# The end of a whole block of an expert, moved from ahead of the branch into both of its arms

## The chip, the cores and the metric

One core of a Trainium2 chip runs the whole program: TensorE (PE, with its weight loads as PEld), VectorE (DVE), ScalarE (ACT), GpSimd (POOL) and the queue of transfers of SyncE (SP). The metric is the device time of one launch in microseconds, the median of several launches.

## The reference

Attention with keys and values that are averaged over 8 rows, then two layers of experts (mixture of experts) over 4608 rows of 512 numbers. The first layer sends each row to its two best of 8 experts, the second to its best one. An expert is two matrix products with a ReLU between them.

```python
def _moe_ref(x, w_gate, w_noise, noise, w1, w2) -> np.ndarray:
    ...
    top2 = np.argpartition(-noisy_logits, 2, axis=1)[:, :2]
    ...
    for e in range(E):
        for k in range(2):
            mask = top2[:, k] == e
            if not mask.any():
                continue
            h = np.maximum(x[mask] @ w1[e], 0.0)
            out[mask] += top2_w[mask, k, None] * (h @ w2[e])

def _moe2_ref(x, w_gate, w_output_gate, w1, w2) -> np.ndarray:
    ...
    e_idx = np.argmax(logits, axis=1)
    ...
        h = np.maximum(x[mask] @ w1[e], 0.0)
        ye = h @ w2[e]
        out[mask] = gate_w[mask, None] * eom[mask, e, None] * ye
```

## The kernel before

The first 250 us are the attention and the routing of the first layer; they are not touched. Then 16 experts run one after the other (k = 0 to 7 in the first layer, 8 to 15 in the second), each through `region(k)`. How many rows an expert has is known only on the chip, so its rows run in **whole blocks** of 256 rows, as nested branches: `level(j)` is the j-th whole block, and `deeper(j)` asks with `tc.If(reg["m"] > more_than(j + 1))` (L1445) whether one more follows. If so, the if-arm holds `level(j + 1)`; if not, the else-arm holds only weight work that is left over (`rest`), or is empty. A remainder of over 192 rows counts as a whole block. Behind all levels three more branches (L1454, L1457, L1460) choose the **part block**: none, or one of up to 64, 128 or 192 rows. The branch at L1445 is announced to PE, ACT, DVE and SP at the start of each whole block by `hint(j)` (L1410); the three of the part block are not announced, and no branch is announced to POOL.

A whole block (`block` with rows == PAIR) stands in this order. `head` copies the rows' places and issues the load and the gather of the next block's rows (`nxt`: SP loads `metaN`, L760, then POOL gathers `xg`, L766). The first layer's product runs in four groups (`m1_pair`, L936), each ended by ACT and DVE (L944, L945). Then come the second product of rows 0 to 127 (`m2(k, 0)`, L998, 24 matmuls), the transposes of the next block's rows (`t_pe`, L868, ended by `t_ev`: L874 on ACT, L875 on DVE), the eviction of the first half (`y_ev`, with a write by POOL, L1027), and then the part that this change is about: the second product of rows 128 to 255 (`m2(k, 1)`, 24 matmuls), beside it on DVE some products with the gate of the second layer (`dot`, L1062, the list `own`), in the second whole block of an expert also the ranks (`rank2`), the row numbers for the write of the second half (`didx`, L1272) and `leave` (ACT L1056, L1057, DVE L1059). The second half itself is evicted at the start of the next block (`y_last`).

The gate products of a block's first half that its own `own` does not reach are done by the next block: `own` holds `OWN[min(j, 2)]` of 8 (3, 4, 6 by level), a whole block starts at `done = OWN[min(j, 3) - 1]`, and a part block at `min(OWN)` = 3, whatever the block ahead did. They are done in the experts 1 to 7 alone.

PE, ACT, DVE and SP run in the order in which the code issues; POOL's order is the scheduler's. Engines wait for each other by counters, one for each engine, that each instruction raises when it is done. The number of raises must be the same on every path through a branch, so that an arm that leaves instructions out raises the counter by what is missing, behind a wait that all earlier work of its own engine is done.

Of the kernel before, what the change touches and what calls it, by code (L numbers as in the profile page):

```python
# [25 lines left out]
E = 8  # L26
# [10 lines left out]
NT = 5  # L37
# [656 lines left out]
PAIR = 256  # L694
# [14 lines left out]
OWN = (3, 4, 6)  # L709


class Weights:
# [64 lines left out]
class Moe(Weights):  # L777
# [353 lines left out]

    def block(self, k, rows, j, nxt, last, extra, places, mid=None, z=True, turned=False):

# [4 lines left out]
        first, calm = j == 0, j > 1  # L1138
        done = OWN[min(j, 3) - 1] if rows == PAIR else min(OWN)
        col = 5 if moe == 0 else 1  # L1140
# [107 lines left out]
        if rows == PAIR:  # L1248
            if nxt is not None:
                if not gate:  # L1250
                    self.t_ev()
                if moe == 1:
                    self.z_dots(e)
            more(places[5])
            if calm:
                more(99, own)
            else:
                more(BEFORE, own)
            self.m2(k, 1, self.t_pe if turned else self.rank2_pe if pend and not calm else None, 7 if turned else 5)
            if turned:  # L1260
                self.t_ev()
                self.z_dots(e)
            if pend and not calm:
                self.rank2(own)
            more(99, own)
        elif rows == PAIR - QUART:
            more(places[5])
            self.m2_rest(w2, 1, self.rank2_pe if pend else None)
            if pend:
                self.rank2(between)  # L1270
            more(99, between)
# [111 lines left out]
    def region(self, k):  # L1383
# [28 lines left out]
        def level(j):  # L1412
# [22 lines left out]
            else:  # L1435
                def some(rows):
                    self.block(k, rows, j, lambda: self.fetch(moe, self.next_row(moe, e, j), self.c.scat[-4 * NT:] if k == 0 and j == 1 else ()), last,
                               plan[j] if j < 2 else [], places.get(j, [0] * 6), mid if first else None)
                if not first:
                    hint(j)  # L1440
                some(PAIR)
            deeper(j)

        def deeper(j):
            with tc.If(reg["m"] > more_than(j + 1), label=f"whole{k}_{j + 1}") as cmp:  # L1445
                level(j + 1)
            rest = sum(plan[j + 1:], [])
            if rest:
                with cmp.Else():
                    for f in rest:  # L1450
                        f()
# [133 lines left out]
```

## Time and profile before

| | |
|---|---|
| runs | 1708.25, 1708.44, 1714.56 us (median 1708.44) |
| profiled execution | 1712.64 us, its span 1710.9 us |
| granted TensorE clock, mean over the span | 0.968 of full speed |
| busy share of the span | PE 94%, PEld 84%, DVE 66%, ACT 41%, POOL 38% |

The page lists for each group of instructions how long its engine was idle just before it and what ended the idle time. "Issue" means that the engine waited for nothing that the profile shows. A q behind an engine's name is its sequencer, which runs ahead of the engine and takes the branches and the waits. A matmul's line has its start, then its duration.

### The profile page before, as it was taken

Reading aid. Unit: us, or ns where it says so; the run is one execution under the profiler, and the core shown is the slowest. Engines: PE = TensorE matmul, PEld = TensorE weight load, DVE = VectorE, ACT = ScalarE, POOL = GpSimd, SP = SyncE. Lnnn points to the kernel's source line nnn. Section 1 sums busy time; section 2 is a strip of 40 time slices with the busy share of each in tenths; the row PEclk is TensorE's granted clock in tenths of the full one; section 3 lists DMA queues with packets and bytes.
Section 4 is the critical chain, followed back from the end, with each engine's and each line's share of the span. In section 5 each row is a group of like instructions: output and inputs, shape, how many; then the busy total and the mean of one; then the engine's idle time right before and its main releaser. Section 6 shows DMA issues by size and latency. Waiting matters only on the chain. (4 is left out here: it accounts for less than half of the span.)

```text
span 1710.9 us, 31718 instructions
## 1 busy us (share of the span) xinstructions
PE 1600.5 (94%) x10551; PEld 1439.3 (84%) x10551; DVE 1121.5 (66%) x3941; ACT 693.4 (41%) x1388; POOL 651.9 (38%) x613
## 2 busy tenths in 40 slices
PE   7988889999999998998998999999999999899997
PEld 6878778899888898888887898888888998798886
DVE  6889874248787886886886887875444534535452
ACT  5766743252442532442532623422343423424242
POOL 4566673144354454353452553542221211112121
PEclk8988999999999999999999999999999999899998
DMA  9977865164281471562551752922423411623231
GB/s 233 266 199 216 229 204 187 58 184 114 66 215 59 120 186 57 135 159 64 154 155 54 191 143 53 248 79 71 137 86 114 147 50 61 192 74 107 91 106 32
DMA packets 148564, 226.48 MB, mean 132 GB/s; under 512 B 45090, under 2 KB 83490, under 8 KB 148128
## 3 DMA queue, kind: packets, MB, share of 16 engines
q1 hardware_dynamic: 104832, 121.67, 24.3%
q0 software_dynamic: 42368, 101.18, 22.2%
q8 instruction: 130, 2.13, 0.5%
q14 instruction: 178, 1.46, 0.3%
q10 hardware_dynamic: 1056, 0.03, 0.0%
HBM read 181.67 MB, written 54.89 MB: 138 GB/s over the span
## 5 line engine op out<-in xcount | busy, mean ns | idle before, releaser
L998 PE MATMUL yps<-w,hT 128*128 128x512 f32 x2616 | 630.7, 393 | 0.0
L936 PE MATMUL hps<-xT,w 128*128 128x256 f32 x4704 | 585.6, 286 | 22.1 <-DVEq L1454 6.8
L936 PEld LDWEIGHTS hps<-xT,w 128*128 128x128 f32 x4704 | 578.9, 194 | 32.1 <-issue 9.6
L998 PEld LDWEIGHTS yps<-w,hT 128*128 128x128 f32 x2616 | 481.5, 188 | 94.0
L1062 DVE SCALAR_TENSOR_TENSOR scr<-yb,gb 128x512 f32<-128x512 f32 x532 | 342.0, 687 | 2.7 <-DVE hT L945 1.8
L945 DVE SCALAR_TENSOR_TENSOR hT<-hps,hT 128x512 fp32r<-128x512 f32 x196 | 135.5, 691 | 229.4 <-ACT hT L944 229.3
L944 ACT ACTIVATE hT<-hps 128x512 fp32r<-128x512 f32 x196 | 117.1, 597 | 413.7 <-PE hps L936 397.5
L1027 POOL DMA_INDIRECT out_dram<-yb,didx x46 | 48.0, 1044 | 367.4 <-ACT yb L1035 306.5
L1027 POOL DMA_INDIRECT X<-yb,didx x80 | 89.4, 1118 | 239.8 <-DVE rk L1122 50.5
L766 POOL DMA_INDIRECT xg<-X,metaN x128 | 143.9, 1124 | 90.2 <-DMA metaN<-meta 36.0
L1128 POOL DMA_INDIRECT meta<-pay,sli x70 | 76.0, 1086 | 228.4 <-DMA meta<-pay,sli 111.4
L875 DVE TENSOR_TENSOR xT<-tps,xT 128x512 fp32r<-128x512 f32 x128 | 83.0, 685 | 118.5 <-ACT xT L874 118.3
L745 ACT ACTIVATE w<-stg 128x1024 fp32r<-128x1024 f32 x128 | 134.3, 1055 | 25.3 <-DMA stg<-in_moe_w_dram 25.1
L956 PE MATMUL hps<-xT,w 128*128 128x256 f32 (+1 forms) x408 | 114.1, 366 | 27.7 <-DVEq L1445 12.1
L956 PEld LDWEIGHTS hps<-xT,w 128*128 128x128 f32 x408 | 82.9, 203 | 33.2 <-issue 33.2
L874 ACT ACTIVATE xT<-tps 128x512 fp32r<-128x512 f32 x128 | 69.8, 595 | 90.3 <-PE tps L868 90.2
L751 DVE TENSOR_TENSOR w<-stg,w 128x1024 fp32r<-128x1024 f32 x68 | 82.6, 1225 | 30.5 <-ACT w L745 30.0
L958 PE MATMUL hps<-xT,w 128*128 128x128 f32 (+1 forms) x408 | 98.8, 242 | 2.2 <-issue 2.2
L529 PE MATMUL po<-Vb,AT 96*128 96x162 f32 (+1 forms) x480 | 81.6, 327 | 17.5 <-DVE Ur L554 13.3
L529 PEld LDWEIGHTS po<-Vb,AT 96*128 96x128 f32 (+1 forms) x480 | 68.5, 193 | 22.6 <-issue 15.7
L958 PEld LDWEIGHTS hps<-xT,w 128*128 128x128 f32 x408 | 84.3, 207 | 2.7 <-issue 2.7
L920 POOL DMA_INDIRECT prow<-X,pidx x70 | 76.8, 1097 | 24.4 <-issue 13.4
(279 smaller groups left out, 1846.5 us busy)
## 6 DMA issues: line engine op xcount, KB each, us to landing
stg<-in_moe_w_dram SPq DMA_DIRECT2D x128, 512.0 KB
w<-in_moe_w_dram POOLq DMA_DIRECT2D x56, 512.0 KB
vst<-in_v_dram SPq DMA_DIRECT2D x16, 576.0 KB
X<-zw SPq DMA_DIRECT2D x36, 256.0 KB
X<-xr SPq DMA_DIRECT2D x32, 256.0 KB
kst<-in_k_dram SPq DMA_DIRECT2D x14, 576.0 KB
qt<-in_q_dram SPq DMA_DIRECT2D x15, 512.0 KB
meta<-zm SPq DMA_DIRECT2D x20, 116.0 KB
```

What stands on the lines that cost most here:

```text
L529: nc.tensor.matmul(po[r, j:j + 2, :], lhsT=at[:, j, r], rhs=Vb[b % 2][:, 3 * hh + j], start=(j == 0), stop=(j == 2), skip_group_check=True)
L745: self.nc.scalar.activation(hi, self.stg[s % n], AF.Copy)
L766: return [nc.gpsimd.indirect_dma_start(out=c.xg[:, i, :], out_offset=None, in_=src, in_offset=bass.IndirectOffsetOnAxis(ap=c.metaN[:, i, 0 ...
L875: f = lambda i=i, hi=hi, lo=lo: self.nc.vector.tensor_sub(lo, self.tps[i], hi.bitcast(F32))
L936: nc.tensor.matmul(ps[:, a, :], lhsT=w[:, wi, kc, f * P:(f + 1) * P], rhs=x, start=(n == 0), stop=(n == 11))
L944: nc.scalar.activation(hi, ps, AF.Relu)
L945: nc.vector.scalar_tensor_tensor(lo, ps, 0.0, hi.bitcast(F32), op0=OP.max, op1=OP.subtract)
L956: nc.tensor.matmul(ps[a], lhsT=w[:, 0, kc, f * P:(f + 1) * P], rhs=x, start=(kc == 0), stop=False, skip_group_check=True)
L958: nc.tensor.matmul(ps[a][:, 0, :], lhsT=w[:, 1, kc, f * P:(f + 1) * P], rhs=x[:, 0, :], start=False, stop=(kc == 3), skip_group_check=True)
L998: self.nc.tensor.matmul(self.yps[i], lhsT=h, rhs=w2[:, wi, f, :], start=(f == n == 0), stop=(f == 7 and n == 2))
L1027: ins = nc.gpsimd.indirect_dma_start(out=c.out if moe else c.X, out_offset=bass.IndirectOffsetOnAxis(ap=self.didx[:, i:i + 1], axis=0), in ...
L1062: self.nc.vector.scalar_tensor_tensor((self.scr[0], self.ya if narrow else self.scr[1])[ex % 2], self.yb[:, i, :], 1.0, self.c.wgb[:, ex, ...
```

## The change

`block` gets an argument `split`. Its part from `more(99 if calm else BEFORE, ...)` to `leave` becomes a function `finish`; with `split` it is not run but returned. Levels with an ordinary whole block (all but the first whole blocks of k = 0 and k = 8, and the loop for levels from 6 on) pass it to `deeper`, which runs it first thing in the if-arm, ahead of the next level, and first thing in the else-arm. In the else-arm `finish(LEFT)` does at most 4 of the `own` products, and a part block now starts at 4 in place of 3.

```diff
+LEFT = 4
...
-    def block(self, k, rows, j, nxt, last, extra, places, mid=None, z=True, turned=False):
+    def block(self, k, rows, j, nxt, last, extra, places, mid=None, z=True, turned=False, split=False):
...
-        done = OWN[min(j, 3) - 1] if rows == PAIR else min(OWN)
+        done = OWN[min(j, 3) - 1] if rows == PAIR else LEFT
...
             more(places[5])
-            if calm:
-                more(99, own)
-            else:
-                more(BEFORE, own)
-            self.m2(k, 1, self.t_pe if turned else self.rank2_pe if pend and not calm else None, 7 if turned else 5)
-            if turned:
-                self.t_ev()
-                self.z_dots(e)
-            if pend and not calm:
-                self.rank2(own)
-            more(99, own)
+            def finish(n=E):
+                mine = own[:n]
+                more(99 if calm else BEFORE, mine)
+                self.m2(k, 1, self.t_pe if turned else self.rank2_pe if pend and not calm else None, 7 if turned else 5)
+                if turned:
+                    self.t_ev()
+                    self.z_dots(e)
+                if pend and not calm:
+                    self.rank2(mine)
+                more(99, mine)
+                nc.vector.tensor_copy(self.didx[:, 1:2], self.metaC[:, 1, col:col + 1])
+                self.leave(moe, e, halves)
+                for f in extra:
+                    f()
+            if split:
+                return finish
+            finish()
+            return
...
-                some(PAIR)
+                return deeper(j, some(PAIR))
             deeper(j)
 
-        def deeper(j):
+        def deeper(j, finish=None):
+
+            rest = sum(plan[j + 1:], [])
             with tc.If(reg["m"] > more_than(j + 1), label=f"whole{k}_{j + 1}") as cmp:
+                if finish:
+                    finish()
                 level(j + 1)
-            rest = sum(plan[j + 1:], [])
-            if rest:
+            if rest or finish:
                 with cmp.Else():
+                    if finish:
+                        finish(LEFT)
                     for f in rest:
                         f()
```

The order of instructions on two engines, for expert 1. In brackets stand the counters that an instruction waits for; `yps_3729` is the accumulator of a block's second half, `tps` and `xg` belong to the next block's rows.

**PE, from the else-arms to the part block, before.** The row with x6 is the six else-arms of the six levels, one branch each to the place behind them; no other shown instruction stands in an arm.

```order
L1445 UNCONDITIONAL_BRANCH [waits PE_49,PE_sequencer_49] x6
L1454 COMPARE_AND_BRANCH
L1457 COMPARE_AND_BRANCH
L956 MATMUL hps_3725<-xT,w_1_3682 128x256 [waits DVE_49,Activation_49]
L958 MATMUL hps_3725<-xT,w_1_3682 128x128
```

**PE, the same place, now.** The last rows of the sixth else-arm (that of the first whole block) and what follows.

```order
L1000 MATMUL yps_3729<-w_1_3683,hT_3686 128x512 x2
L1000 MATMUL yps_3729<-w_1_3683,hT_3687 128x512
L1000 MATMUL yps_3729<-w_1_3683,hT_3686 128x512
L1457 UNCONDITIONAL_BRANCH [waits PE_sequencer_49]
L1469 COMPARE_AND_BRANCH
L1472 COMPARE_AND_BRANCH
L958 MATMUL hps_3725<-xT,w_1_3682 128x256 [waits DVE_49,Activation_49]
L960 MATMUL hps_3725<-xT,w_1_3682 128x128
```

Each else-arm now holds the 24 matmuls of the second half, and its branch no longer waits for PE's own counter: the first matmul of the arm raises it by what is missing.

**PE, at the end of a level, now.** Transposes of the next block's rows, then the branch.

```order
L870 MATMUL tps_3724<-identf,xg 128x128 [waits DMASW6_49]
L870 MATMUL tps_3724<-identf,xg 128x128 x3
L1457 COMPARE_AND_BRANCH
L1000 MATMUL yps_3729<-w_1_3683,hT_3686 128x512
L1000 MATMUL yps_3729<-w_1_3683,hT_3687 128x512
```

The branch stands ahead of the second half's matmuls, where it stood behind them.

**DVE, at the end of a level, before.** L1023 is the eviction of the first half, L1062 a gate product.

```order
L1023 SCALAR_TENSOR_TENSOR yb<-prow,metaC,ya 128x512 [waits DMASW0_49,Activation_49]
L1062 SCALAR_TENSOR_TENSOR scr_3696,lg_3702<-yb,gb 128x512 [waits DVE_49]
L1062 SCALAR_TENSOR_TENSOR scr_3697,lg_3702<-yb,gb 128x512
L1062 SCALAR_TENSOR_TENSOR scr_3696,lg_3702<-yb,gb 128x512 [waits DVE_49]
L1062 SCALAR_TENSOR_TENSOR scr_3697,lg_3702<-yb,gb 128x512 [waits DVE_49]
L1062 SCALAR_TENSOR_TENSOR scr_3696,lg_3702<-yb,gb 128x512 [waits DVE_49]
L1062 SCALAR_TENSOR_TENSOR scr_3697,lg_3702<-yb,gb 128x512 [waits DVE_49]
L1272 COPY didx<-metaC 128x1 [waits DMASW5_49]
L1059 MEMSET pidx 128x2 [waits DMASW1_49]
L1445 COMPARE_AND_BRANCH
```

**DVE, an else-arm of a third or later whole block, now.** The branch L1457 of the level stands right behind the eviction of the first half (L1025).

```order
L1064 SCALAR_TENSOR_TENSOR scr_3696,lg_3702<-yb,gb 128x512 [waits DVE_49]
L1064 SCALAR_TENSOR_TENSOR scr_3697,lg_3702<-yb,gb 128x512
L1064 SCALAR_TENSOR_TENSOR scr_3696,lg_3702<-yb,gb 128x512 [waits DVE_49]
L1064 SCALAR_TENSOR_TENSOR scr_3697,lg_3702<-yb,gb 128x512 [waits DVE_49]
L1268 COPY didx<-metaC 128x1 [waits DMASW4_49]
L1061 MEMSET pidx 128x2 [waits DMASW1_49]
L1457 UNCONDITIONAL_BRANCH [waits DVE_sequencer_49]
```

Six products ahead of the branch have become four in the arm behind it (six in the if-arm). The branch at the arm's end, which waited for DVE's own counter before, waits for it no longer, and the arm's first product raises the counter by what is missing.

## Rows read from the trace of the kernel before

**Rows 1.** The page: busy us of the engines, share of the span, instructions.

```profile
PE 1600.5 (94%) x10551; PEld 1439.3 (84%) x10551; DVE 1121.5 (66%) x3941; ACT 693.4 (41%) x1388; POOL 651.9 (38%) x613
```

**Rows 2.** The page's costliest groups: busy us, mean ns | idle before, releaser.

```profile
L1062 DVE SCALAR_TENSOR_TENSOR scr<-yb,gb 128x512 f32<-128x512 f32 x532 | 342.0, 687 | 2.7 <-DVE hT L945 1.8
...
L956 PE MATMUL hps<-xT,w 128*128 128x256 f32 (+1 forms) x408 | 114.1, 366 | 27.7 <-DVEq L1445 12.1
```

**Rows 3.** Instructions of L956, the sequencer's wait ahead of a part block's first matmul.

```profile
L956 PEldq EVENT_SEMAPHORE  x14: 51/51/51, 331.9 to 1653.6; - x14
```

**Rows 4.** Timeline of PE, part block of expert 3: start, us, ..., [idle before].

```profile
675.53 0.66 PE L956 MATMUL hps<-xT,w 128*128 128x384 f32 x1 [4.33 <-issue]
...
676.15 0.58 PE L956 MATMUL hps<-xT,w 128*128 128x384 f32 x1
...
676.68 0.57 PE L956 MATMUL hps<-xT,w 128*128 128x384 f32 x1
...
680.86 0.36 PE L956 MATMUL hps<-xT,w 128*128 128x384 f32 x1
...
681.15 0.36 PE L956 MATMUL hps<-xT,w 128*128 128x384 f32 x1
...
696.66 0.17 PE L1113 MATMUL rps<-ohb,tri 128*128 128x16 bf16 x1 [0.72 <-DVE ohb L1095]
```

**Rows 5.** Instructions of L1445, 665.5 to 677 us: ns min/median/max, first and last start.

```profile
L1445 PEldq COMPARE_BRANCH  x2: 184/270/355, 667.0 to 671.5; - x2
...
L1445 DVEq COMPARE_BRANCH  x2: 47/64/80, 670.6 to 673.6; - x2
L1445 PEldq EVENT_SEMAPHORE  x2: 51/51/51, 671.2 to 671.4; - x2
L1445 DVEq EVENT_SEMAPHORE  x2: 21/21/21, 673.4 to 673.5; - x2
```

**Rows 6.** Instructions of L1460 in the same stretch.

```profile
L1460 PEldq COMPARE_BRANCH  x1: 2976/2976/2976, 672.4 to 672.4; - x1
```

**Rows 7.** Windows: us, busy PE, PEld, DVE, ACT, POOL, granted clock, DMA, GB/s.

```profile
673.91:680.74 6.83, 5.21 (x19) 5.24 (x20) 2.26 (x7) 0.66 (x2) 2.39 (x3) 0.50 0.14 46
...
919.67:926.50 6.83, 4.99 (x19) 4.99 (x20) 2.33 (x7) 0.66 (x2) 2.23 (x2) 0.50 0.14 46
```

**Rows 8.** Timeline of PE at the exits of experts 1, 5 and 12.

```profile
443.21 0.36 PE L956 MATMUL hps<-xT,w 128*128 128x256 f32 x1 [2.39 <-DVEq L1445]
...
918.86 0.41 PE L956 MATMUL hps<-xT,w 128*128 128x384 f32 x1 [2.41 <-DVEq L1445]
921.51 0.53 PE L958 MATMUL hps<-xT,w 128*128 128x192 f32 x1 [2.24 <-issue]
...
1547.56 0.36 PE L956 MATMUL hps<-xT,w 128*128 128x256 f32 x1 [1.06 <-ACT zc L907]
```

**Rows 9.** Timeline of DVE at the exit of expert 3.

```profile
667.22 0.74 DVE L1023 SCALAR_TENSOR_TENSOR yb<-prow,metaC,ya 128x512 f32<-128x512 f32 x1
...
671.77 0.06 DVE L1059 MEMSET pidx<- 128x2 int32 x1
675.91 0.18 DVE L892 COPY metaP<-metaC 128x16 int32<-128x16 int32 x1 [4.08 <-issue]
```

**Rows 10.** Waits of the whole span: us in total, times, longest.

```profile
PEld tps L868 <- DMA xg<-X,metaN: 11.2, 11, 3.2
```

**Rows 11.** Timeline of DVE at the exit of expert 12.

```profile
1545.07 0.15 DVE L1272 COPY didx<-metaC 128x1 int32<-128x1 int32 x1
1547.45 0.15 DVE L894 COPY scP<-sc 128x1 f32<-128x1 f32 x1 [2.23 <-ACT zc L907]
```

**Rows 12.** Instructions of L1454 in the last expert, 1694 to 1703 us.

```profile
L1454 PEldq COMPARE_BRANCH  x1: 3360/3360/3360, 1698.9 to 1698.9; - x1
```

**Rows 13.** Timelines of ACT and of POOL, the last instruction of each.

```profile
1702.47 0.69 ACT L1035 ACTIVATE yb<-yps,scP 128x512 f32<-128x512 f32 x1 [8.01 <-PEq L1454]
...
1703.43 1.01 POOL L1027 DMA_INDIRECT out_dram<-yb,didx  x1 [9.17 <-ACT yb L1035]
```

More of the change, by code (lines that the diff above doesn't have):

```diff
@@ L1436, in some @@
                 def some(rows):
-                    self.block(k, rows, j, lambda: self.fetch(moe, self.next_row(moe, e, j), self.c.scat[-4 * NT:] if k == 0 and j == 1 else ()), last,
-                               plan[j] if j < 2 else [], places.get(j, [0] * 6), mid if first else None)
+                    return self.block(k, rows, j, lambda: self.fetch(moe, self.next_row(moe, e, j), self.c.scat[-4 * NT:] if k == 0 and j == 1 else ()), last,
+                                      plan[j] if j < 2 else [], places.get(j, [0] * 6), mid if first else None, split=True)
                 if not first:
                     hint(j)
-                some(PAIR)
+                return deeper(j, some(PAIR))
             deeper(j)
-        def deeper(j):
+        def deeper(j, finish=None):
+            rest = sum(plan[j + 1:], [])
             with tc.If(reg["m"] > more_than(j + 1), label=f"whole{k}_{j + 1}") as cmp:
+                if finish:
+                    finish()
                 level(j + 1)
-            rest = sum(plan[j + 1:], [])
-            if rest:
+            if rest or finish:
                 with cmp.Else():
+                    if finish:
+                        finish(LEFT)
                     for f in rest:
```

## The prediction

> **What bounds the kernel now.** I read the page first. TensorE is busy for 94% of the span and no other engine for more than two thirds [rows 1], so time is to be had where PE stands still or runs at half clock. Of the page's costliest groups I looked next for those with much idle time ahead of them. The first matmul of a part block (L956) stands out: 27.7 us of idle time [rows 2], and 14 of the 16 experts run a part block [rows 3], so PE stands still for 2 us on average between the last whole block of an expert and its part block. From whole block to whole block it does not.
>
> The timeline shows one such exit, that of expert 3: PE idles 4.33 us, and "issue" says that it waited for no other engine [rows 4]. The branches explain it. PE's sequencer takes the branch behind the whole block at 667.0 us, but its next instruction, the counter event of the else-arm, stands at 671.2 [rows 5], when the last matmul of the second half is done. So the sequencer runs 4.2 us ahead of the array, and throws that lead away because the else-arm waits for all of PE's work. After that everything is paid with an empty array: two counter events, the jump at 671.5 [rows 5], L1454 and L1457, and then L1460, which takes 2.98 us [rows 6], against 0.18 to 0.36 us of the taken branches at L1445 [rows 5]: the code of the 192-row block had to be loaded first. Before the first matmul PE also waits for counters of DVE and ACT; at expert 1 that was the later end, 2.39 us [rows 8]. DVE too takes a branch late: at 670.6, behind its gate products, and its first event in the arm is at 673.4 [rows 5], though its work was done at 671.8 [rows 9].
>
> The gap has a second price. At the exits of experts 3, 4 and 5 the granted clock is 0.50 for a stretch of 6.83 us, of which PE works 5.2 and 5.0 us in the first and last [rows 7]; a pair of matmuls takes 0.53 us there (676.15 to 676.68) and 0.29 us after it (680.86 to 681.15) [rows 4]. Those are 1.2 and 2.4 GHz, and what came before the fall was the idle stretch.
>
> **The change part by part.** (1) *The branch ahead of the second half, on PE.* Its sequencer now takes the branch while first-half matmuls and transposes are still queued, issues the 24 matmuls of the arm, and finds no wait for its own work behind them. With the lead of 4.2 us it passes the jump and the three branches while the array works. At expert 3 these cost 671.2 to 675.5, the whole 4.3 us; that just fits, with nothing to spare. The gap that is left is 0 to 0.5 us. I count the three long exits first: 4.33 us at expert 3, one like it at expert 4, 2.41 + 2.24 us at expert 5 [rows 4, 8]: 13.3 us. Without the gap the clock has no reason to fall: three times 5.2 us at half clock would take 0.29/0.53 of it, which gives back 2.4 us each, 7.1 us. Together 20.4 us, 6.8 us an exit.
>
> Whether these are kept is DVE's to say, since a 192-row block ends with PE waiting 0.72 us for DVE's ranks [rows 4]. DVE gets three things: three gate products fewer in each of these exits (two in the arm, one in the part block) at a start-to-start of about 0.61 to 0.69 us ([rows 2], 687 ns each), 1.8 to 2.1 us; a branch that it takes right behind L1023, at about 667.5 in place of 670.6, so that its code load (2.8 us, [rows 5]) begins 3 us earlier and part of its idle 4.08 us [rows 9] goes; and less waiting inside, for in the half-clock stretch it is busy only 2.26 of 6.83 us [rows 7]. That is 1.8 + about 2 + up to 4.6, over the 6.8 that PE wants. I take 6.3 us an exit, **19 us**; the bounds are 4 (what DVE surely gives) and 6.8 each, 12 to 20.4.
>
> (2) *The other part blocks.* 27.7 less the 11.1 us of the three exits leaves 16.6 us for 11 exits, 1.5 us each. Five are in the first layer (7.5 us). There DVE and PE both pass sooner, but short part blocks end on the gather of the next rows, for which PE waits 11.2 us at 11 places [rows 10]. That chain (copy of `metaN` on DVE, load by SP, gather by POOL) starts when DVE is through its own branches, and POOL, to which no branch is announced, is no earlier. I take half, **4 us**, between 1 and 7.5. Six exits are in the second layer (9.1 us). There `own` is empty and the products with the output gate stand ahead of the branch as before, so DVE takes its branch at the same time; at expert 12 it is done with its work at 1545.2 and comes to the next block at 1547.45 [rows 11]. PE's first matmul still waits for DVE's first instruction in the arm, so that of 1.06 us [rows 8] about half goes, and the gather ends no earlier. I take **1 us** of 9.1, between 0 and 5.
>
> (3) *The end of the program.* Expert 15 has no part block: PE takes L1454 at 1698.9 with an empty array and needs 3.36 us for it [rows 12]; ACT's last eviction waits for that 8.01 us in all and starts at 1702.47, POOL's last write follows at 1703.43 [rows 13]. Now PE takes this branch in its lead. I take **2.5 us**, between 0 and 3.4, for DVE and POOL have branches of their own there. At expert 11, also without a part block, DVE passes last; I take 0, between 0 and 3.
>
> (4) *What the if-arms cost.* Between whole blocks the branch is not taken away but moved ahead of the same instructions, which fall through; PE has no idle time there now, and its lead of 4.2 us [rows 5] covers a branch. POOL's order changes by a few places (the gather of the next rows stands ahead of the write of the last half), at the start of a block at whose end the rows are needed. I take nothing, and at most 2 us either way.
>
> The sum is 19 + 4 + 1 + 2.5 = 26.5 us. From the profiled execution's 1712.6 that leaves 1686.1; this execution stands 4.2 us over the median 1708.44, so the forecast is 1682 us. With all terms at their lower bounds the gain is 13 us (1695), with all at their upper ones about 41 us (1667).
>
> **The rivals.** *DVE takes PE's place.* The first matmul of a part block waits for the counter that the arm's first gate product raises. If DVE's code load starts no earlier than now, that product ends at about 674 in place of 671.2, PE idles 2.8 us in place of 4.3, and the clock still falls: term (1) shrinks to 3 times 1.5 us, and with half of (2) and (3) the gain is about 9 us, 1699 us. For it speaks that DVE is named as the releaser at experts 1 and 5 [rows 8]; against it, that the products no longer stand ahead of DVE's branch.
>
> *The branches get longer: slower.* The else-arms grow on PE from one jump to 24 matmuls with their weight loads, so that an exit from the fourth whole block has some 150 more instructions to jump over, behind the arm and ahead of the part block. If that makes a second code load of 3 us [rows 6] necessary at an exit, 4.2 us of lead no longer cover them: 7 us against 4.2, so 2.8 us and a fallen clock (2.4 us) at each of the 14 exits, 73 us, where gaps and half clock cost 37 us now (27.7 + 2.2 + 7.1). That is up to 36 us slower, and with such a second load at every other exit nothing is won. I set this case halfway between the two, at 1725 us. It decides from the second load at one exit on. Against it: the announced branch at L1445 is taken in 0.36 us [rows 5], with its arm just as far away as the part block is, so that loading ahead works there, and a load can run while the arm's 24 matmuls are issued.
>
> The Trainium skill has a rule for this case, in "Runtime: NRT & Kernel Launch", section "Instruction fetch mechanics": code streams in blocks of 256 instructions, and a taken branch to a place outside the loaded blocks stops the engine until that block has been fetched. The 2.98 us at L1460 agree with it; the 0.36 us at L1445 show that an announced branch escapes it. By that rule alone the longer arms would add stops, and the time would be this rival's.
>
> *The change does not do what it says.* If PE's sequencer cannot run past the arm, for instance because the queue is full of the arm's own matmuls until they are done, the exits stay as they are, and only the gate products that lie beside PE's work go: 0 to 4 us, 1706 us. Against it stands the lead of 4.2 us, measured with the same 24 matmuls in the queue [rows 5].
>
> **How the numbers follow.** Forecast 0.72 (1682 us, its own range 1667 to 1695), DVE in PE's place 0.12 (1699), longer branches 0.08 (1725), no effect 0.08 (1706). A measurement here can tell about 0.5%, 8.5 us, from no change, so faster means below 1699.9. Faster takes the forecast and half of the second case, 0.78; the same the other half and the last, 0.14; slower the third, 0.08. The range reaches from 1667 to 1704: it leaves out the slower rival and little more at either end.
>
> **What would show it.** Right: after the change the idle time ahead of the first matmul of part blocks (now L958) falls from 27.7 us to under 10; at expert 3 the branches L1469 to L1475 stand before the last matmul's end, and the stretches at clock 0.50 behind experts 3, 4 and 5 are gone; the gate products (L1064) number about 511 in place of 532. DVE's part: PE's wait for the ranks stays under 1.5 us. The second layer's exits should keep about their time. Wrong: a PE branch that takes 3 us or more twice at one exit, PE's first matmul released by DVE at most exits, or idle time that comes up again at the transposes (L870) in the size of what was saved.

## The result, and the profile after

| | before | changed |
|---|---|---|
| median | 1711.36 us (4 runs) | 1684.96 us (4 runs, 1681.21 to 1685.89) |
| ratio, 95% interval | | 0.9839, 0.9817 to 0.9861 |
| profiled execution | 1712.64 us | 1685.89 us, its span 1684.2 us |

The forecast was 1682 us, 26.5 us below the median that the kernel before had then (1708.44 us, 3 runs); by the medians of the table it is 26.4 us. The range held, but the agreement to a tenth is luck: the interval stands for 24 to 31 us, and two of the terms missed in opposite directions. Lines stand two further down than before up to L1132: L956 is L958, L1062 is L1064; L1445 is L1457, and the part block's branches are L1469, L1472, L1475.

The page after, engines and groups with busy us, mean ns | idle before, releaser. They answer [rows 1, 2].

```profile
PE 1594.6 (95%) x10551; PEld 1433.2 (85%) x10551; DVE 1105.5 (66%) x3899; ACT 692.6 (41%) x1388; POOL 651.8 (39%) x613
...
L1064 DVE SCALAR_TENSOR_TENSOR scr<-yb,gb 128x512 f32<-128x512 f32 x514 | 330.4, 686 | 17.6 <-issue 15.1
...
L958 PE MATMUL hps<-xT,w 128*128 128x256 f32 (+1 forms) x408 | 106.4, 350 | 8.5 <-DVE scr L1064 3.6
```

The idle time ahead of a part block's first matmul fell from 27.7 to 8.5 us; 6.7 us of the rest stand at experts 2 and 4 and 1.7 at expert 14. DVE has 42 instructions fewer: 21 gate products (18 of the form shown, 3 that write to another tile), each with its read of the sum. New is DVE's own idle time: 17.6 us ahead of the products, 15.1 of them "issue", where it was 2.7 in all.

The exit of expert 3, instructions of L1457, L1472 and L1475 on PE's sequencer (ns min/median/max, first and last start), against [rows 5, 6]:

```profile
L1457 PEldq COMPARE_BRANCH  x2: 198/276/355, 664.7 to 668.9; - x2
L1472 PEldq COMPARE_BRANCH  x1: 414/414/414, 669.3 to 669.3; - x1
L1475 PEldq COMPARE_BRANCH  x1: 3077/3077/3077, 669.8 to 669.8; - x1
```

Timeline of PE there, against [rows 4]:

```profile
672.16 0.84 PE L1000 MATMUL yps<-w,hT 128*128 128x512 f32 x3
673.06 0.41 PE L958 MATMUL hps<-xT,w 128*128 128x384 f32 x1
...
673.39 0.36 PE L958 MATMUL hps<-xT,w 128*128 128x384 f32 x1
...
691.71 0.17 PE L1115 MATMUL rps<-ohb,tri 128*128 128x16 bf16 x1 [0.67 <-DVE ohb L1097]
```

Windows behind the exits of experts 3 and 5 (us, busy PE, PEld, DVE, ACT, POOL, granted clock, DMA, GB/s), against [rows 7]:

```profile
673.00:680.00 7.00, 6.94 (x49) 6.97 (x50) 5.59 (x23) 2.47 (x7) 2.12 (x2) 1.00 0.17 52
...
909.00:916.00 7.00, 7.00 (x51) 7.00 (x51) 5.59 (x23) 2.52 (x8) 1.16 (x2) 1.00 0.16 49
```

The same code load as before, 3.08 us in place of 2.98, runs while the last matmuls of the second half do; the array passes to the part block without a pause. The clock stays at 1.00, and DVE is busy for 5.59 of 7 us where it had 2.26 of 6.83. PE's wait for the ranks stayed at 0.67 us, from 0.72.

At experts 2 and 4 it is otherwise. L1472 and L1475 at expert 2, then at expert 4, and PE's first matmul there:

```profile
L1472 PEldq COMPARE_BRANCH  x1: 3162/3162/3162, 549.5 to 549.5; - x1
L1475 PEldq COMPARE_BRANCH  x1: 3226/3226/3226, 552.7 to 552.7; - x1
L1472 PEldq COMPARE_BRANCH  x1: 3411/3411/3411, 786.6 to 786.6; - x1
L1475 PEldq COMPARE_BRANCH  x1: 3471/3471/3471, 790.1 to 790.1; - x1
...
556.09 0.41 PE L958 MATMUL hps<-xT,w 128*128 128x384 f32 x1 [3.09 <-DVE yb L1041]
793.72 0.41 PE L958 MATMUL hps<-xT,w 128*128 128x384 f32 x1 [3.60 <-DVE scr L1064]
```

Two loads follow each other, 6.4 and 6.9 us against a lead of 4.2. That these branches load code is in the trace's transfers: in each of the four, one packet of 16 KB of an instruction queue starts 0.5 to 1.2 us after the branch. The windows of the two branches at expert 2 (549.48 to 552.64 and 552.70 to 555.90 us), queue and kind: packets, MB, share of 16 engines:

```profile
q8 instruction: 1, 0.02, 2.2%
...
q8 instruction: 1, 0.02, 2.3%
```

In the 14 traces of this case, each of the 156 branches of 2.5 us or more that PE's sequencer takes at an exit has such a packet starting within it. The releaser in the bracket misleads: DVE had raised its counter long before (at expert 4 the arm's first product ended at 789.6), and PE's sequencer came last. This is the mechanism of the rival "the branches get longer", at 2 exits of 14.

### The profile page after: what moved, and what is told of

It reads as the page before. It is cut to its first block, busy times and chain, and to the rows that moved or that the text cites. A ratio compares the mean times of both kernels' runs of the same rounds, so it can differ in the third digit from the quotient of the medians.

```text
span 1684.2 us, 31668 instructions
## 1 busy us (share of the span) xinstructions
PE 1594.6 (95%) x10551; PEld 1433.2 (85%) x10551; DVE 1105.5 (66%) x3899; ACT 692.6 (41%) x1388; POOL 651.8 (39%) x613
## 3 DMA queue, kind: packets, MB, share of 16 engines
q14 instruction: 184, 1.51, 0.3%
## 5 line engine op out<-in xcount | busy, mean ns | idle before, releaser
L938 PEld LDWEIGHTS hps<-xT,w 128*128 128x128 f32 x4704 | 579.0, 194 | 29.7 <-issue 8.8
L1064 DVE SCALAR_TENSOR_TENSOR scr<-yb,gb 128x512 f32<-128x512 f32 x514 | 330.4, 686 | 17.6 <-issue 15.1
L958 PE MATMUL hps<-xT,w 128*128 128x256 f32 (+1 forms) x408 | 106.4, 350 | 8.5 <-DVE scr L1064 3.6
L958 PEld LDWEIGHTS hps<-xT,w 128*128 128x128 f32 x408 | 78.8, 193 | 11.1 <-issue 10.8
L507 ACT ACTIVATE A<-ps,nm 128x72 f32<-128x72 f32 x288 | 68.0, 319 | 42.2 <-DVE nm L496 41.5
L418 POOL DMA_INDIRECT meta<-pay,r_sli x70 | 67.8, 969 | 43.5 <-DVE pay L413 19.6
```

Source lines behind the costliest of these rows:

```text
L938: nc.tensor.matmul(ps[:, a, :], lhsT=w[:, wi, kc, f * P:(f + 1) * P], rhs=x, start=(n == 0), stop=(n == 11))
L958: nc.tensor.matmul(ps[a], lhsT=w[:, 0, kc, f * P:(f + 1) * P], rhs=x, start=(kc == 0), stop=False, skip_group_check=True)
L1064: self.nc.vector.scalar_tensor_tensor((self.scr[0], self.ya if narrow else self.scr[1])[ex % 2], self.yb[:, i, :], 1.0, self.c.wgb[:, ex, ...
```

## Where the time went, expert by expert

Single executions differ by up to 3 us in one expert, because a stretch at half clock falls here or there. So I averaged traces, with some of the experiments below. First layer, as changed: the changed kernel, its repeat, the shifted one and the one with the first layer alone; as before: the kernel before, its shifted form, and the one with the second layer alone. Second layer, as changed: the changed kernel, its repeat, the shifted one; as before: the kernel before, its shifted form, and the one with the first layer alone. "Gap" is the time from the start of the last matmul of the whole blocks to the part block's first, "part" from there to the next expert's first matmul, both in us. For experts 11 and 15 the gap goes to the next expert's first matmul and to the end of the span.

| experts | gap, change | part, change | sum | taken in the prediction (bounds) |
|---|---|---|---|---|
| 3, 4, 5 | -4.57, -1.55, -2.55 | -2.44, -1.83, -4.40 | -17.3 | -19 (-12 to -20.4) |
| 0, 1, 6, 7 | -1.64, -2.57, -1.44, -1.30 | +0.54, +1.83, +0.64, +2.28 | -1.7 | with expert 2: -4 (-1 to -7.5) |
| 2 | +1.57 | +0.33 | +1.9 | |
| 8, 9, 10, 12, 13, 14 | -1.13, -1.38, -1.11, -1.17, -1.41, -0.65 | +0.01, -0.61, -0.06, +0.11, -1.26, -0.56 | -9.2 | -1 (0 to -5) |
| 15 | -2.49 | | -2.5 | -2.5 (0 to -3.4) |
| 11 | -1.50 | | -1.5 | 0 (0 to -3) |

The sum is 30 us, 4 more than the medians say. Two of the profiled executions stood at the ends of their kernels' runs (the shifted form of before 6.7 us above its median, the shifted changed kernel 7.8 us below), so that the table shows where the time went and not how much to a microsecond. The longest pause that is left stands at expert 11, which has no part block: PE idles 5.63 us there in the changed kernel's trace (6.85 before). Its own branch L1469 ended 3.5 us ahead of its next matmul; it waits for DVE's:

```profile
1456.33 0.98 PE L938 MATMUL hps<-xT,w 128*128 128x256 f32 x3 [5.63 <-DVEq L1469]
```

## The experiments

**One layer alone.** My first reading of the two single traces, expert by expert, gave the second layer more than the first. Two kernels split the change by layer.

```diff
-            if split:
+            if split and moe == 0:
                 return finish
```

The second has `moe == 1` there, and part blocks that start at 3 again.

> Only the experts 1 to 7 (first layer) get the changed end of a whole block; the second layer is as before. By the terms on record the first layer brings 19 + 4 = 23 us of the 26.5, so about 1688 us where the kernel before takes 1711. By the two traces, laid side by side expert by expert, it brings only about 10 us (experts 3, 4 and 5 win 16.5 us, the experts with a shorter part block lose 6.7 us together), so about 1701 us.

> Only the experts 8 to 15 (second layer) get the changed end; the first layer is as before, with part blocks that start at 3 products. By the terms on record (1 us for six exits, 2.5 us for the end) it is 3.5 us faster, about 1708 us against 1711. By the two traces laid side by side it brings about 15 us, of which 1.1 to 1.4 us is each exit's gap, so about 1696 us. It leaves out nothing of the computation.

First layer alone: 1690.43 us against 1708.39, ratio 0.9882 (0.9864 to 0.9900). Second layer alone: 1702.50 us, 0.9964 (0.9950 to 0.9978). So 18 and 6 us: the forecasts 1688 and 1708 were nearer than what I had read from the single traces (1701, 1696), though the first layer brings less than its terms (18 in place of 23) and the second more (6 in place of 3.5). The second layer alone has a handicap that the changed kernel has not, slow branches of DVE at three of its exits; this is taken up below.

**PE's part ahead of the branch again.** This tells the sequencer's lead from DVE's share.

```diff
+            def half():
+                self.m2(k, 1, self.t_pe if turned else self.rank2_pe if pend and not calm else None, 7 if turned else 5)
+            if split:
+                half()
             def finish(n=E):
                 mine = own[:n]
                 more(99 if calm else BEFORE, mine)
-                self.m2(k, 1, self.t_pe if turned else self.rank2_pe if pend and not calm else None, 7 if turned else 5)
+                if not split:
+                    half()
```

> The 24 matmuls of the second half stay ahead of the branch; VectorE's and ScalarE's part stands in the arms as in the changed kernel, with its fewer products. TensorE's else-arm is empty again and waits for TensorE's own counter. If the lead of its sequencer brings the time, nearly all of the gain goes: the exits' 25 us of standing still and the clock behind the long ones come back, 1704 to 1711 us. If VectorE's earlier branch and fewer products bring it, most of the gain stays: 1686 to 1695 us.

1702.91 us, ratio 0.9967 (0.9953 to 0.9982): 5.5 us of the 26 are left. The exit of expert 3 in this kernel (its L1462 is L1457, L1480 is L1475), counter events and branches of the two sequencers, then PE's first matmul of the part block:

```profile
L1462 PEldq EVENT_SEMAPHORE  x2: 51/51/51, 670.2 to 670.3; - x2
...
L1480 PEldq COMPARE_BRANCH  x1: 2976/2976/2976, 671.3 to 671.3; - x1
L1480 DVEq COMPARE_BRANCH  x1: 63/63/63, 671.4 to 671.4; - x1
...
674.46 0.66 PE L958 MATMUL hps<-xT,w 128*128 128x384 f32 x1 [4.33 <-DVE scr L1064]
```

DVE is through its last branch at 671.4, 3.1 us ahead of PE's first matmul, with two products fewer than before; PE waits 4.33 us as in [rows 4], to the hundredth, since its sequencer takes the load of 2976 ns with an empty array. So DVE is not what the long exits waited for. The lead is. One thing this run does not separate: it puts back the branch behind the matmuls and the else-arm's wait for PE's own counter, both at once. The sequencer of before also took its branch at 667.0 and lost its lead in that wait [rows 5], so a kernel that keeps the branch in its place and drops the wait alone might win as much on PE. It was not run.

**All gate products.** The move without `LEFT`.

```diff
-        done = OWN[min(j, 3) - 1] if rows == PAIR else LEFT
+        done = OWN[min(j, 3) - 1] if rows == PAIR else min(OWN)
...
-                        finish(LEFT)
+                        finish()
```

> The branch is moved as in the changed kernel, but the else-arm does all of its gate products (up to 6) and a part block starts at 3 of 8 again: 3 products more for VectorE at most exits of the first layer. If the lead of TensorE's sequencer is what brings the time, at most VectorE's share is lost: 0 to 6 us slower than the changed kernel, 1685 to 1691 us. If fewer products are what brings it, seven exits of about 2 us come back and more where the clock falls: about 1700 us.

1690.53 us, ratio 0.9896 (0.9877 to 0.9914), between the two expectations: 7 to 10 us above the changed kernel. So the move without the fewer products brings 16 to 18 us (this run and its repeat below), the fewer products and DVE's earlier branch without PE's part 5.5, both together 23 to 26. With intervals of some 3 us on each of these, it is not shown that the two are worth more together than apart. Nor are the 7 to 10 us the price of the products alone: in this kernel DVE's branches at three exits of the second layer, where no gate product runs, take 3 us in place of 0.7. By the traces, the exits of the first layer are some 5 us longer than in the changed kernel and those of the second 3 to 4.

**The long body first.** If distance makes the second load at experts 2 and 4, the body of 192 rows must stand nearest. This kernel, the next two and a repeat of the changed kernel ran on a chip on which the kernel before takes 1770.27 us, so ratios count; in the traces of the changed kernel, 49 us of the difference lie ahead of the first expert.

```diff
-            with tc.If(reg["sf"] < QUART) as cm2:
-                some(QUART)
+            with tc.If(reg["sf"] > P - 1) as cm2:
+                some(PAIR - QUART)
             with cm2.Else():
-                with tc.If(reg["sf"] < P) as cm3:
-                    some(P)
+                with tc.If(reg["sf"] < QUART) as cm3:
+                    some(QUART)
                 with cm3.Else():
-                    some(PAIR - QUART)
+                    some(P)
```

> The changed kernel once more, unaltered, beside the three that follow, so that each has it on the same chip: 1685 us, 1.6% faster than the kernel before.

> The changed kernel with the bodies of the part block in another order: the one of 192 rows stands first, those of 64 and 128 rows behind it. In the changed kernel TensorE's sequencer loads code twice at the exits of experts 2 and 4 (3.16 + 3.23 and 3.41 + 3.47 us), both with a part block of 192 rows whose body stands behind the other two, and gaps of 3.1 and 3.6 us are left there. If the distance to that body makes the second load, both gaps go, with some half clock: 6 to 8 us faster than the changed kernel, 1677 to 1679 us. If the loads only move to the exits with short part blocks, where each is a single one under the lead of 4.2 us, nothing is lost either; if they come twice there, the time stays at 1685 us or rises by up to 4 us.

The changed kernel: 1744.78 us, 0.9855 (0.9829 to 0.9881). With the long body first: 1749.90 us, 0.9880 (0.9855 to 0.9906), not faster. The gaps at experts 2 and 4 did go (from 3.6 and 3.4 us to 0.2 and 0.4, start to start), so the second load came with the place of the body. Distance is not all of it: in the changed kernel, the exits of experts 3 and 5 lead to the same body in the same order and take one load each. And the loads came up elsewhere. L1472 and L1475 at expert 6 (a part block of at most 128 rows), PE's first matmul there, and the next expert's first whole block behind the 192-row block of expert 3:

```profile
L1472 PEldq COMPARE_BRANCH  x1: 4003/4003/4003, 1082.2 to 1082.2; - x1
L1475 PEldq COMPARE_BRANCH  x1: 2965/2965/2965, 1086.3 to 1086.3; - x1
...
1089.42 0.55 PE L958 MATMUL hps<-xT,w 128*128 128x256 f32 x1 [3.68 <-DVE scr L1064]
...
755.29 2.98 PE L938 MATMUL hps<-xT,w 128*128 128x256 f32 x23 [1.51 <-DVE metaC L897]
```

Expert 6 now has the two loads, and at the end of the long body PE must jump over the other two. That branch takes 3.32 us, where the changed kernel's takes 0.18: 1.51 us of idle time ahead of the next expert, where the changed kernel has 0.50. The first expectation held for its place and fell for the total.

**DVE's bare load.** DVE's idle 15.1 us stand between the first half's eviction and the arm's products, as here at expert 7 of the changed kernel:

```profile
1135.26 0.74 DVE L1025 SCALAR_TENSOR_TENSOR yb<-prow,metaC,ya 128x512 f32<-128x512 f32 x1
1138.24 0.69 DVE L1064 SCALAR_TENSOR_TENSOR scr<-yb,gb 128x512 f32<-128x512 f32 x1 [2.24 <-issue]
...
1141.60 0.75 DVE L1041 SCALAR_TENSOR_TENSOR yb<-yps,metaP,pb 128x512 f32<-128x512 f32 x1
```

Before, products stood ahead of the branch and covered the load. At this exit DVE came to the eviction of the last half (before L1039, now L1041) 0.8 us behind the part block's first matmul, now 2.5. Two kernels try to cover the load: one takes the branch ahead of both evictions, the other puts two products ahead of it.

```diff
+        def evict():
+            if rows == PAIR and gate and nxt is not None:
+                self.t_ev()
+            if rows != PAIR - QUART:
+                self.y_ev(moe, e, 0, self.metaC, self.sc[:, 0, :])
+        if not (split and gate):
+            evict()
...
                 mine = own[:n]
+                if split and gate:
+                    evict()
```

```diff
+            if split:
+                more(2, own)
             def finish(n=E):
-                mine = own[:n]
+                mine = own[:max(n - 2, 0)]
```

> The changed kernel, with the branch of the first layer's levels still earlier: ahead of the eviction of the next rows' transposes and of the first half, so that ScalarE and VectorE take it some 1.5 us sooner, and TensorE as now. In the changed kernel VectorE stands still for 15.1 us in all ahead of the arms' products, 2.2 us at each of seven exits. If that decides the short part blocks of experts 1, 6 and 7, which are 2 to 4 us longer than before, it brings 4 to 6 us: 1679 to 1681 us. If TensorE alone decides, the time stays within 2 us of 1685.

> The changed kernel with two of VectorE's gate products back ahead of the branch and the others in the arms (two in the else-arm, up to four in the if-arm), so that 1.3 of the 2.2 us for which VectorE stands still at an exit of the first layer are covered by work. If that standing still is what the short part blocks of experts 1, 6 and 7 pay, 2 to 4 us come back: 1681 to 1683 us. If it hides beside TensorE's work, the time is that of the changed kernel, 1685 us; if two products delay VectorE's branch by as much, it is so too, and the idle time shows it (15.1 us would stay).

Earlier branch: 1746.85 us, 0.9873 (0.9848 to 0.9898), the same within the interval. Two products ahead: 1752.14 us, 0.9892 (0.9870 to 0.9914), slower: each of its six runs lies above all six of the changed kernel. The products' groups of the two, in that order:

```profile
L1064 DVE SCALAR_TENSOR_TENSOR scr<-yb,gb 128x512 f32<-128x512 f32 x514 | 330.7, 687 | 2.9 <-DVE hT L947 1.1 <-issue 0.9
L1064 DVE SCALAR_TENSOR_TENSOR scr<-yb,gb 128x512 f32<-128x512 f32 x514 | 329.5, 687 | 18.8 <-issue 16.3 <-DVE hT L947 1.6
```

Two products ahead hide nothing: the branch comes later by as much as they take, the idle time stays at 16.3 us, and PE now waits 0.7 to 1.2 us more at five exits of the first layer, because the arm's first product comes later. The earlier branch does remove the idle time, and the part block of expert 1 becomes shorter: 16.07 us, from 18.09 in the first trace of the changed kernel and 19.67 on this chip, where it has some half clock. Those of experts 6 and 7 stay (17.0 and 18.7 us, from 17.1 and 18.6 on this chip). Over the first layer's exits, gaps and part blocks, it won 5.1 us by the two traces; 3.3 us of that were lost in the second layer, whose source is the same in both: at experts 8, 9, 12 and 13 a gap of about 1 us came back. DVE's branch there (L1462 in this kernel) takes 3.0 us; in the changed kernel (L1457) 0.7. In all traces, each branch of DVE of 2.9 us or more at these exits has a packet of 8 KB of an instruction queue that starts 1.0 to 1.3 us after it, and the quick ones at expert 13 have none; so the slow ones load code. Expert 13, first the earlier branch, then the changed kernel, each with DVE's branches and the arm's first event, then PE's first matmul:

```profile
L1462 DVEq COMPARE_BRANCH  x2: 47/64/80, 1643.1 to 1646.2; - x2
L1462 DVEq EVENT_SEMAPHORE  x1: 21/21/21, 1646.1 to 1646.1; - x1
1646.35 0.35 PE L958 MATMUL hps<-xT,w 128*128 128x256 f32 x1 [0.73 <-DVE didx L1273]
...
L1457 DVEq COMPARE_BRANCH  x2: 47/70/92, 1588.3 to 1589.0; - x2
L1457 DVEq EVENT_SEMAPHORE  x1: 21/21/21, 1588.9 to 1588.9; - x1
1590.62 0.28 PE L958 MATMUL hps<-xT,w 128*128 128x256 f32 x1
```

**Does the place of the code decide?** The next four moved DVE's code of the second layer without a change to it, by small writes in a loop that no expert of this data reaches: 162 in the changed kernel, 94 with the earlier branch, 307 in the kernel before, 179 with all products.

```diff
+        self.unused = T([P, 1], I32, name="unused")
...
+                    if k == 7:
+                        for _ in range(162):
+                            nc.vector.memset(self.unused, 0)
                     self.block(k, PAIR, LEVELS, nxt, e, [], [0] * 6)
```

> The changed kernel with 162 small writes of VectorE added in the loop for levels from 6 on of expert 7, which no expert of this data reaches: not one executed instruction differs, but VectorE's code of the second layer lies 162 places further on, as in the kernel with the earlier branch, where VectorE's branch at the second layer's exits took 3.0 us in place of 0.66. If the place of the code alone decides whether an announced branch finds its code loaded, five or six exits pay about 0.8 us of gap and experts 9 and 13 some 1 us more: 4 to 6 us slower than the changed kernel, a ratio to the kernel before of about 0.988. If the longer arms or the number of waits ahead of the branch decide it, the ratio is the changed kernel's, 0.984 to 0.9855.

> The kernel with the branch of the first layer's levels ahead of the evictions, and 94 such writes that never run, which put VectorE's code of the second layer 256 places on from where the changed kernel has it. If places count in steps of that size, the second layer's exits are quick again and what the earlier branch brings in the first layer (2 to 4 us at experts 1 and 7) is left: a ratio of 0.981 to 0.983, faster than both kernels. If the earlier branch brings nothing, 0.985; if the place does not decide, 0.987 as it was without the writes.

> The kernel before with 307 such writes that never run, so that VectorE's code of the second layer lies where it did when only the first layer was changed (there its branch at the second layer's exits took 1.3 us, in the kernel before 2.8 us, and the part blocks of experts 9 and 13 were 1.8 to 2.0 us shorter). If the place of the code decides, the kernel before gets 3 to 5 us faster, 0.997 to 0.998, without any change of an executed instruction, and that much of the second layer's gain was no merit of the moved branch. If not, 1.000.

> The moved branch with all gate products (up to 6 in the else-arm, part blocks from 3 on), and 179 such writes that never run, which put VectorE's code of the second layer 256 places on from where the changed kernel has it. Without them this kernel stood at 0.9896, but its branches at the second layer's exits were slow. If the place decides, 2 to 5 us of that go and the rest is the price of the products alone: 0.987 to 0.988. If it does not, the time stays at 0.9896 and the products cost all of it.

| kernel | us (before: 1707.69) | ratio, 95% interval |
|---|---|---|
| changed, shifted by 162 | 1681.48 | 0.9855, 0.9832 to 0.9878 |
| earlier branch, 94 | 1678.54 | 0.9816, 0.9793 to 0.9840 |
| before, 307 | 1710.88 | 1.0013, 0.9999 to 1.0027 |
| all products, 179 | 1691.28 | 0.9914, 0.9886 to 0.9942 |

The theory fell. The changed kernel stays as fast with its code shifted as in the kernel with the slow branches; the kernel before gains nothing where the code lies as in the one with quick branches; the kernel with all products has its branches slow although its writes were counted to put its code 256 places on from where the changed kernel has it. Expert 13 in the shifted changed kernel and in the one with all products, DVE's branches (L1461 in both) and PE's first matmul:

```profile
L1461 DVEq COMPARE_BRANCH  x2: 47/70/92, 1576.3 to 1577.1; - x2
1578.63 0.28 PE L959 MATMUL hps<-xT,w 128*128 128x256 f32 x1
...
L1461 DVEq COMPARE_BRANCH  x2: 47/64/80, 1588.1 to 1591.1; - x2
1591.27 0.36 PE L959 MATMUL hps<-xT,w 128*128 128x256 f32 x1 [0.68 <-DVE didx L1269]
```

What they do show is the link: where DVE's announced branch takes 0.7 us, PE passes without a pause, and where it takes 3 us, PE waits about 0.7 us for the arm's first instruction on DVE. Both the quick branch and the lead are needed: the kernel with PE's part ahead again has quick branches at the exits of experts 8, 9, 10, 12 and 13, and its gaps there are those of before (1.33 to 1.61 us).

What the quick branches are worth is less sure. The six exits of the second layer, gap and part block together, take 94.3 to 96.4 us in the changed kernel and its two like, all with quick branches; 98.6 to 99.9 us in the five kernels with the changed second layer and slow branches at three or four of the exits (the second layer alone among them); 107 us in the kernel before. But the earlier branch with 94 writes takes 98.2 us with quick branches, and the kernel with the first layer alone 100.4 us with the second layer's source of before, its branches at 1.4 to 2.1 us. So 3 to 5 us is a difference of two groups of single traces that nearly touch; it may be why the second layer alone brought only 6. What decides between quick and slow stays open; it is not the place of DVE's code by itself. The earlier branch with 94 writes has the lowest ratio of all, but its interval overlaps with that of the changed kernel, which took 1681.48 us beside it in its shifted form: 3 us that these runs can't tell from none. The second run with all products stands 10 us above the changed kernel, again with slow branches in the second layer.

## Why the prediction was right, point by point

*The lead of PE's sequencer* carried it. It was read from one branch at 667.0 and the next event at 671.2 [rows 5], and at experts 3 and 5 it covers the load as forecast: 7.0 us an exit, where 6.8 was the most that I allowed. The half clock went with the gap. The step that failed at expert 4 is "with nothing to spare": I priced the exits by the loads that the trace of before showed there, one at experts 3 and 4 and none at 2, and set a second load at one exit down as a rival for all exits at once (1725 us). It came at experts 2 and 4 alone: 3.4 us in place of 6.3 at expert 4 and 1.9 us lost at expert 2. The mechanism was seen, and its count was not. Expert 2 stood in the wrong term besides: its part block has 192 rows too (128x384 above), and I had counted it with the short ones.

The Trainium skill, "Runtime: NRT & Kernel Launch", section "Instruction fetch mechanics", says that a taken branch to a place outside the loaded code stops the engine until that code has come. The 3.16 and 3.23 us in a row at expert 2 agree with it, as does the jump over the bodies in the kernel with the long one first; what it would make of the whole, the rival's time, did not come, because a single load fits under the lead.

*DVE's share.* The trace after stands 1.8 us later at this place, so times count from the start of the first half's eviction, 667.22 before [rows 9] and 669.01 now. The branch forecast "right behind L1023, at about 667.5" stood at 668.88, 0.1 us ahead of that start, where it had been 3.4 us behind it. Timeline of DVE at expert 3, against [rows 9]:

```profile
669.01 0.74 DVE L1025 SCALAR_TENSOR_TENSOR yb<-prow,metaC,ya 128x512 f32<-128x512 f32 x1
671.87 0.69 DVE L1064 SCALAR_TENSOR_TENSOR scr<-yb,gb 128x512 f32<-128x512 f32 x1 [2.11 <-issue]
...
674.39 0.17 DVE L894 COPY metaP<-metaC 128x16 int32<-128x16 int32 x1
```

DVE came to the first instruction of the part block 5.4 us behind that start, before 8.7: 3.3 us sooner. Of its idle time of 4.08 us, 2.11 us are left, and they have moved ahead of the products. The long part blocks have room for that; the short ones do not.

*The first layer's other exits* (4 us taken, between 1 and 7.5): about 0. Their gaps fell by 7.0 us in experts 0, 1, 6 and 7, as the branch step said, and 5.3 us came back inside the part blocks. At expert 1 the traces show what was late. PE's idle time inside its part block, in the changed kernel and then before; last, the waits for the gather over the whole span of the changed kernel, against [rows 10]:

```profile
446.98 1.06 PE L1080 MATMUL rps<-wg,scr 128*128 128x8 f32 x8 [0.57 <-ACT scr L1074]
450.77 0.66 PE L870 MATMUL tps<-identf,xg 128*128 128x128 f32 x4 [0.83 <-DMA xg<-X,metaN]
452.21 0.66 PE L870 MATMUL tps<-identf,xg 128*128 128x128 f32 x4 [0.79 <-DMA xg<-X,metaN]
...
452.96 0.66 PE L868 MATMUL tps<-identf,xg 128*128 128x128 f32 x4 [0.43 <-DMA xg<-X,metaN]
...
PEld tps L870 <- DMA xg<-X,metaN: 14.0, 15, 3.4
```

It idles for 2.19 us in place of 0.43, and 1.62 of that end with the gather, which I had named as what would be late next; the sum over the span rose from 11.2 to 14.0 us. With the earlier branch of DVE and ACT, 0.36 us are left at expert 1, so the lateness begins with their branch there. At experts 6 and 7 that kernel changed nothing, and what made their part blocks longer stays open. With the loss at expert 2 the term is below its lower bound.

*The second layer's exits* (1 us, between 0 and 5): 9.2 us by the traces; with slow branches, and the end of the program in it, 6 us by the runs of the second layer alone. The step that failed is "PE's first matmul still waits for DVE's first instruction in the arm, so that ... about half goes". DVE does come to its branch at the same time, but at experts 9, 12 and 13 the branch took 0.7 us in place of 2.9, so that the arm's first instruction is there when PE arrives and the whole gap goes. "The second layer's exits should keep about their time" was wrong. Since no run shows what made the branch quick, the size of this term is in part luck.

*The end.* 2.49 us for 2.5. Last instructions of ACT and POOL, against [rows 13]:

```profile
1675.13 0.69 ACT L1037 ACTIVATE yb<-yps,scP 128x512 f32<-128x512 f32 x1 [5.39 <-DVE scP L1569]
...
1676.76 1.01 POOL L1029 DMA_INDIRECT out_dram<-yb,didx  x1 [7.22 <-ACT yb L1037]
```

PE's load of 3.7 us is hidden, and ACT now waits for DVE in place of PE's sequencer.

Of the four signs, idle time under 10 us (8.5), branches ahead of the last matmul's end at expert 3, full clock behind 3 and 5, and the wait for ranks came; behind expert 4 the averaged traces still have 2.6 of 6.8 us at half clock. The count was 514 for 511, because 3 of the 21 products that went are of another form. But one of the signs of being wrong came too, "a PE branch that takes 3 us or more twice at one exit", at experts 2 and 4. And the lower end of the gain leaves out the 2 us that term (4) allowed either way: it should read 11 us, not 13.

## What to carry to other kernels

A sequencer's lead over its engine is time that a branch may use for nothing: put the branch ahead of the last work that both arms share, and take away whatever waits in an arm for the engine's own earlier work. Count the code loads that fit into the lead at each exit, not only whether one fits, and look on every engine for the work that covered a load before, because moving the branch ahead of that work lays it bare. Judge places by several executions: one pair of traces put the gain into the wrong layer.

## What was not expected of the hardware

A code load at a part block's branch took 2.6 to 4.0 us on PE's sequencer, and on DVE 2.1 to 2.2 us of idle time behind an eviction of 0.74 us. Whether an announced branch needs one changes with edits elsewhere: DVE's branch at the exit of expert 13 took 0.7 us in five kernels and 2.9 to 3.3 us in seven others, five of which have the same instructions in and around it. Unannounced branches cost two loads in a row at some exits (3.16 + 3.23 us) and one at others that lead to the same body, and another order of the bodies moved the pair to another exit.
